# Gated attention and two feed-forward stages on one core: another written order for the first phase

## The chip, the cores and the metric

The program runs on one core of one Trainium2 chip. The core has a matrix engine (PE, with its weight loads shown as PEld), a vector engine (DVE), a scalar engine (ACT), a general engine (POOL) and a queue that issues transfers (SP). Each works through its own list of instructions in order; they meet only where one waits for a semaphore of another. The metric is the device time of one execution in microseconds (us), as the median of several; lower is better.

## The reference

Three stages follow each other. The first is an attention-like recurrence (an mLSTM cell) over 2 batches, 8 heads, 768 time steps and a head size of 40. Its output becomes 1536 tokens of 320 features. They go through a layer of four experts (320 to 1024 to 320), and then through a gated layer (320 to 1536 to 320).

```
for t in range(S):                                    # per batch b and head h
    m_new = max(f[t] + m, i[t])
    C = exp(f[t] + m - m_new) * C + exp(i[t] - m_new) * outer(v[t], k[t])
    n = exp(f[t] + m - m_new) * n + exp(i[t] - m_new) * k[t]
    y[t] = sigmoid(o[t]) * (C @ q[t]) / max(|n . q[t]|, 1)
x   = y as (B*S, H*D)
x   = sum over e of p[:, e] * (relu(x @ w1[e]) @ w2[e])        # p: normalised domain_probs
out = ((x @ w_a) * (x @ w_b)) @ w_out
```

## The kernel before

**Tiling.** The 768 steps are cut into six chunks (j = 0 to 5) of 128 steps. With two batches that gives twelve token tiles n = 2j and 2j + 1, each of 128 tokens. Every f32 operand of a matmul in the two feed-forward stages is split into a high half and a low half, and three products are added. The weights come in pieces: a piece is loaded, ACT copies its high half (L88), and POOL or DVE computes its low half (L90).

**Phase one** is what the change touches. It mixes two kinds of work on PE. One is the first expert blocks of the second stage, in *items*: 12 items for each chunk, numbered k = 0, 1, 2 and so on. An item's first part `a()` runs eight matmuls into `psa` (L201). ACT then evicts them as `hh` (L218, the high half), and DVE as `hl` (L219, the low half). Its second part `b()`, three matmuls per token tile into `psy` (L242 to L244), follows two items later. There are two `psa` buffers, so item k + 2 cannot start before DVE has done the `hl` of item k. Expert sums leave `psy` as `acc`: by ACT in the first blocks (L251), by DVE later (L253).

The other kind is the attention of the next chunk, in *events*. Chunk j is computed while the items of chunk j - 1 run, so what chunk 1 and the start of chunk 2 need runs beside the items of chunk 0, numbered 0 to 11. The events are:

- `gate1` to `gate4` and `gate_tail` compute the gates of a chunk: running maxima and sums by scans on DVE (L338 to L355), their high halves `zh` (`gate_hi`, L360 and L361), the low parts `LT` and `zx` (L367, L368), exponentials `ex` on ACT (L375, L376), a small product `eb` on POOL (L380), and on PE a transpose of `ex` (L386) and a product with `eb` (L389).
- `build_R` fills the right operand `Rr` of the gate products (L398). `weights_of` multiplies (L407), takes the exponential on ACT (L408) and masks it by a select on POOL (L409). `scores` multiplies queries by keys (L417). `s1b` multiplies the two on DVE (L425).
- `s2a` multiplies by the values (L435) and by the old state (L441). `s2b` normalises the result on DVE (L451 to L464) and leaves `x_t`. `weigh_k` (POOL, L473) and `state` (PE L485, DVE L487, POOL L490 and L491) carry the state `cbd` on.
- `s3a` transposes `x_t` on PE (L138 to L140). The third transpose reads the last 64 columns twice, so ACT copies them first (L496). `s3b` or `split_hi` and `split_lo` split the result into `xh` and `xl`, which the items read.
- `table` loads the table of the exponential or of the sigmoid on ACT (L526), and `o_gate` takes the sigmoid (L315).

**The order** of all this is written by hand and not moved by a scheduler. A list `ev` holds pairs of a time and an event. The loop over the items runs all events up to k, then the first part of item k, then the events up to k + 0.5, then the second part of item k - 2, then those up to k + 0.99:

```
for k in range(NI * NCH):
    until(k)
    stream.push(Item(...), lambda: until(k + 0.5))
    until(k + 0.99)
```

Every engine gets its instructions in the order in which this loop emits them. For the chunks 2 to 5 the events come from one list with an offset of 12 per chunk (`new`).

After phase one (from about 210 us) PE runs the remaining expert blocks and the gated layer without attention work.

Of the kernel before, what the change touches and what calls it, by code (L numbers as in the profile page):

```python
# [13 lines left out]
AF = mybir.ActivationFunctionType  # L14
# [3 lines left out]
DM = H * D  # L18
# [28 lines left out]
def mlstm_moe_kernel(ctx, tc, gates, qk, qc, kvo, dp, w1b, w2b, ident_d, bdmask_d, rsel_d, exp_d, out):  # L47
    nc = tc.nc
# [22 lines left out]
    def piece1(i, s, pool, lo_eng, apart=False):  # L71


        if s == 0:
            wblk[i] = (pool.tile([P, WB1], F32R, tag="wh", name=f"wh{i}"), pool.tile([P, WB1], F32R, tag="wl", name=f"wl{i}"))
        wh, wl = wblk[i]
        st = WB1 // NP1
        cs = slice(s * st, (s + 1) * st)
        if i < 3:
            at = (s if i == 0 else 8 + s if s < 2 else s) * st  # L80
            raw = sums[:, at:at + st]
        else:
# [46 lines left out]
    def split_hi(ps, c, o):  # L129
        nc.scalar.copy(xh[c][:, :, o:o + P], ps)  # L130
# [130 lines left out]
    with ExitStack() as c1:  # L261
# [7 lines left out]
        td = {}  # L269
# [61 lines left out]
        def gate1(j, eng):  # L331
            mr = a2.tile([G, P + 1], F32, tag="mr", name="mr")
            if j == 0:
                nc.gpsimd.memset(mr[:, 0:1], NEG)
            else:
                nc.scalar.copy(mr[:, 0:1], g_sb[j - 1]["mr"][:, P:])
            f, ig, m = g_sb[j]["gt"][:, 0], g_sb[j]["gt"][:, 1], mr[:, 1:]
            nc.vector.tensor_tensor_scan(m, f, ig, mr[:, 0:1] if j == 0 else g_sb[j - 1]["mr"][:, P:], op0=ALU.add, op1=ALU.max)  # L338
            cm = a2.tile([G, P], F32, tag="cm", name="cm")
            lf = a2.tile([G, P], F32, tag="lf", name="lf")  # L340
            eng.tensor_tensor(lf, f, mr[:, 0:P], op=ALU.add)
            eng.tensor_tensor(lf, lf, m, op=ALU.subtract)
            eng.tensor_tensor(cm[64:G], ig[64:G], m[64:G], op=ALU.subtract)
            g_sb[j].update(cm=cm, lf=lf, mr=mr)
# [133 lines left out]
        def state(n):  # L478
# [55 lines left out]
        w0, w1, w2 = ([piece1(i, f, wp0, nc.vector if LOENG[i][f] == "v" else nc.gpsimd) for f in range(NP1)] for i in range(3))  # L534
        V = nc.vector
# [56 lines left out]
        for n in range(2):  # L592
# [28 lines left out]
        go(w1[2:6])

        ev = [
            (0.5, gate2, 1), (0.5, gate_hi, 1, nc.vector.tensor_copy), (0.5, table, AF.Exp), (0.6, go, w0[7:]), (0.7, go, w0[6:]), (0.8, go, w1[6:]), (0.9, gate_tail, 0),
            (1.5, gate3, 1), (1.5, build_R, 2, V, 0, 4), (1.6, gate4, 1), (1.8, go, w1[0:2]), (1.9, go, w1[0:2]),
            (2.5, build_R, 2, V, 4, 8), (2.5, weigh_k, 0), (2.7, go, w2[:2]), (2.8, gate_tail, 1), (2.8, go, w1[2:4]), (2.9, go, w1[2:4]), (2.9, scores, 2, 0),
            (3.0, weigh_k, 1), (3.2, weights), (3.5, scores, 2, 1), (3.5, build_R, 3, V, 0, 4), (3.8, go, w1[4:6]), (3.9, weights_of, 2, 0), (3.9, go, w1[4:6]), (3.9, go, w2[2:4]),
            (4.5, weights_of, 2, 1), (4.5, build_R, 3, V, 4, 8), (4.6, table, AF.Sigmoid), (4.7, go, w1[6:8]), (4.8, s1b, 2, 0), (4.8, go, w1[6:8]), (4.9, o_gate, 1), (4.9, go, w2[4:6]),
            (5.0, state, 0), (5.2, go, w2[0:2]), (5.3, table, AF.Exp), (5.4, s1b, 2, 1), (5.4, go, w2[0:2]), (5.45, state, 1), (5.45, load_kvo, 3), (5.5, s2a, 2, 0), (5.6, s2a, 2, 1), (5.9, s2b, 2), (5.9, scores, 3, 0), (5.9, weights_of, 3, 0), (5.9, go, w2[6:8]), (5.95, go, w2[2:4]),
            (6.0, weigh_k, 2), (6.1, go, w2[2:4]), (6.4, gate1, 2, V), (6.6, go, w2[4:6]), (6.8, go, w2[4:6]), (6.9, s1b, 3, 0),  # L630
            (7.0, scores, 3, 1), (7.0, weights_of, 3, 1), (7.4, s3a, 2), (7.4, go, w2[6:8]), (7.45, gate2, 2), (7.5, weigh_k, 3), (7.6, go, w2[6:8]), (7.9, s1b, 3, 1), (7.9, s3b, 2),
            (8.3, gate_hi, 2, nc.scalar.copy), (8.5, s2a, 3, 0), (8.6, s2a, 3, 1), (8.9, s2b, 3),
            (9.4, state, 2), (9.5, gate3, 2), (9.9, state, 3), (10.0, build_R, 4, nc.gpsimd), (10.2, gate4, 2), (10.6, s3a, 3), (10.9, s3b, 3), (10.9, gate_tail, 2), (11.0, build_R, 5, nc.gpsimd),
        ]
# [207 lines left out]
```

## Time and profile before

| what | value |
|---|---|
| median of 3 runs | 647.97 us (647.9 to 648.02) |
| the profiled execution: device time | 647.9 us |
| the profiled execution: span of the trace | 646.2 us |
| PE busy | 626.6 us (97%) |
| PE weight loads busy | 568.6 us (88%) |
| DVE, ACT, POOL busy | 419.9 us (65%), 267.2 us (41%), 182.6 us (28%) |

The span runs from the first to the last instruction; the device time is 1.7 us longer. A row of the timeline gives the start and the length in us, the engine, the line of the kernel, the operation, output and inputs, and how many instructions of this kind follow each other there. A bracket at its end gives how long the engine stood idle before it, and what it waited for. Idle time of PE is the time to look for.

### The profile page before, as it was taken

What the parts mean: (1) busy time and instruction counts of PE and PEld (TensorE: products, weight loads), DVE (VectorE), ACT (ScalarE), POOL (GpSimd) and SP (SyncE); (2) the same over time, 40 slices, a digit from 0 to 9 for tenths busy, and PEclk for the clock granted to TensorE, in tenths of its full rate; (3) what the DMA queues carried; (4) which work ended last, traced back from release to release, by engine and by line L of the source; (5) the groups of instructions that cost most, each with busy time, mean ns of one, the idle gap of its engine ahead of it and who ended that gap; (6) DMA issues with size and microseconds to landing.
All of it is one profiled execution on the core that took longest, in us unless ns stands there. A gap on an engine that the chain in (4) does not pass through costs nothing.

```text
span 646.2 us, 10283 instructions
## 1 busy us (share of the span) xinstructions
PE 626.6 (97%) x3798; PEld 568.6 (88%) x3799; DVE 419.9 (65%) x860; ACT 267.2 (41%) x592; POOL 182.6 (28%) x217
## 2 busy tenths in 40 slices
PE   8887999999999999999999999999999999999997
PEld 6787989999999999999888988888888888888886
DVE  8986858576654244323587888888766776764343
ACT  6774454453614333232343443454544433332221
POOL 4595242525101111233243333322121222220000
PEclk9997999999999999999999999999999999999999
DMA  7873152615201122223122221211111111000003
GB/s 225 241 230 92 40 129 55 166 55 153 71 1 47 44 57 77 59 79 100 45 69 58 65 69 53 71 53 52 36 51 30 43 50 37 18 0 2 1 9 115
DMA packets 27487, 45.99 MB, mean 71 GB/s; under 512 B 3189, under 2 KB 17773, under 8 KB 27437
## 3 DMA queue, kind: packets, MB, share of 16 engines
q1 hardware_dynamic: 27437, 45.33, 25.2%
q8 instruction: 30, 0.49, 0.3%
q14 instruction: 20, 0.16, 0.1%
HBM read 43.35 MB, written 1.97 MB: 70 GB/s over the span
## 4 chain that ended last, share of the span: by engine, by line
PE 90%; DVE 5%; ACT 2%; issue 1%; POOL 1%; DVEq 0%; ACTq 0%; POOLq 0%
PE psa L201 37%; PE psy L242 12%; PE psy L244 11%; PE psy L243 11%; PE psb L201 10%; PE pt_y L435 3%; PE pt_c L417 2%; PE pt_i L441 1%; PE pt_a L407 1%; PE pt_u L485 1%; PE pt_e L389 1%; PE pt_x L140 1%; ACT hh L218 0%; ACT qs_t L301 0%; ACT acc L251 0%
## 5 line engine op out<-in xcount | busy, mean ns | idle before, releaser
L242 PE MATMUL psy<-wh,hh 128*128 128x320 f32 x528 | 166.3, 315 | 1.7 <-ACT acc L251 1.7
L244 PE MATMUL psy<-wh,hl 128*128 128x320 f32 x528 | 163.2, 309 | 0.0
L243 PE MATMUL psy<-wl,hh 128*128 128x320 f32 x528 | 163.1, 309 | 0.0
L201 PE MATMUL psa<-xh,wh 128*128 128x512 f32 (+1 forms) x504 | 149.6, 351 | 1.7 <-DVE hl L219 1.3
L201 PE MATMUL psa<-xh,wl 128*128 128x512 f32 (+1 forms) x504 | 147.1, 346 | 0.0
L219 DVE SCALAR_TENSOR_TENSOR hl<-psa,hh 128x256 fp32r<-128x256 f32 (+1 forms) x132 | 71.7, 543 | 111.7 <-ACT hh L218 111.2
L218 ACT ACTIVATE hh<-psa 128x256 fp32r<-128x256 f32 (+1 forms) x132 | 63.4, 480 | 187.4 <-PE psa L201 185.8
L242 PEld LDWEIGHTS psy<-wh,hh 128*128 128x128 f32 x528 | 99.8, 189 | 8.5 <-ACT acc L251 2.3
L243 PEld LDWEIGHTS psy<-wl,hh 128*128 128x128 f32 x528 | 99.6, 189 | 4.1
L201 PEld LDWEIGHTS psa<-xh,wl 128*128 128x128 f32 x504 | 90.2, 189 | 12.6
L244 PEld LDWEIGHTS psy<-wh,hl 128*128 128x128 f32 x528 | 99.4, 188 | 0.0
L201 PEld LDWEIGHTS psa<-xh,wh 128*128 128x128 f32 x504 | 89.1, 189 | 9.6 <-DVE hl L219 1.5
L201 PE MATMUL psa<-xl,wh 128*128 128x512 f32 (+1 forms) x336 | 88.9, 346 | 0.0
L122 POOL TENSOR_TENSOR wl<-tp,lf 128x272 fp32r<-128x272 f32 x48 | 38.8, 809 | 124.0 <-DVE tp L121 124.0
L201 PEld LDWEIGHTS psa<-xl,wh 128*128 128x128 f32 x336 | 58.4, 189 | 8.2
L228 DVE TENSOR_TENSOR g<-psa,bs 128x512 f32<-128x512 f32 x36 | 24.9, 691 | 50.2 <-PE psa L201 50.2
L119 POOL TENSOR_TENSOR lf<-lf,sq 128x272 f32<-128x272 f32 x48 | 37.5, 782 | 70.3 <-ACT wh L118 39.6
L90 POOL TENSOR_TENSOR wl<-raw,wh 128x352 fp32r<-128x352 f32 x28 | 26.4, 951 | 97.3 <-ACT wh L88 84.3
L229 ACT CAST hh<-g 128x512 fp32r<-128x512 f32 x36 | 22.3, 621 | 72.3 <-DVE g L228 72.3
L409 POOL TENSOR_SCALAR_AFFINE_SELECT w_t<-w_t 128x512 f32<-128x512 f32 x24 | 17.9, 752 | 83.0 <-ACT w_t L408 56.0
L230 DVE TENSOR_TENSOR hl<-g,hh 128x512 fp32r<-128x512 f32 x36 | 24.9, 693 | 24.7 <-ACT hh L229 24.7
L224 ACT COPY bs<-psb 128x512 f32<-128x512 f32 x36 | 21.2, 588 | 44.0 <-PE psb L201 43.9
(118 smaller groups left out, 893.0 us busy)
## 6 DMA issues: line engine op xcount, KB each, us to landing
raw<-in_w2b SPq DMA_DIRECT2D x48, 272.0 KB, 2.7
qk_t<-in_qk SPq DMA_DIRECT2D x16, 480.0 KB, 6.5
raw<-in_w1b SPq DMA_DIRECT2D x40, 176.0 KB, 2.3
acc<-in_w1b SPq DMA_DIRECT2D x24, 176.0 KB, 3.6
kvo_t<-in_kvo SPq DMA_DIRECT2D x10, 364.5 KB, 5.1
og_t<-in_kvo SPq DMA_DIRECT2D x6, 320.0 KB, 6.5
out<-acc SPq DMA_DIRECT2D x12, 160.0 KB, 1.8
qc_t<-in_qc SPq DMA_DIRECT2D x10, 180.0 KB, 3.1
```

The lines of the kernel that those rows point to most:

```text
L90: lo_eng.tensor_tensor(wl[:, cs], raw, wh[:, cs].bitcast(F32), op=ALU.subtract)
L119: nc.gpsimd.tensor_tensor(lf, lf, sq, op=ALU.mult)
L122: nc.gpsimd.tensor_tensor(wl[:, cs], tf, lf, op=ALU.add)
L201: nc.tensor.matmul(ps, l, r, start=(i == 0), stop=(i == len(prs) - 1))
L218: nc.scalar.activation(self.hh, ps, AF.Relu)
L219: nc.vector.scalar_tensor_tensor(self.hl, ps, 0.0, self.hh.bitcast(F32), op0=ALU.max, op1=ALU.subtract)
L228: nc.vector.tensor_tensor(g, ps, bs, op=ALU.mult)
L229: nc.scalar.copy(self.hh, g)
L230: nc.vector.tensor_tensor(self.hl, g, self.hh.bitcast(F32), op=ALU.subtract)
L242: nc.tensor.matmul(ps, lh, wh[:, off:off + DM], start=(fi == 0), stop=False)
L243: nc.tensor.matmul(ps, lh, wl[:, off:off + DM], start=False, stop=False)
L244: nc.tensor.matmul(ps, ll, wh[:, off:off + DM], start=False, stop=(fi == nf - 1))
```

## The change

Only phase one's written order changes. The copy of the last 64 columns of `x_t` becomes an event of its own, `s2c`, ahead of the transposes. The gate events of chunk 1 move behind the evictions of items 0 and 1, and those of chunk 2 from between two `s1b` steps to places next to them. `weigh_k(1)`, the mask of tile 3 and the product `eb` of chunk 2 move ahead of other work of POOL; `build_R(3)` moves behind other work of DVE. In chunks 2 to 5 the exponential's table is loaded an item earlier, right behind the sigmoid.

```diff
+        def s2c(n):
+            x = td[n]["x"]
+            nc.scalar.copy(x[:, DM:], x[:, 256:DM])
+
         def s3a(n):
             x = td[n]["x"]
-            nc.scalar.copy(x[:, DM:], x[:, 256:DM])
...
-        gate1(1, V)
...
-            (0.5, gate2, 1), (0.5, gate_hi, 1, nc.vector.tensor_copy), (0.5, table, AF.Exp), ...
+            (0.4, gate1, 1, V), (1.45, gate2, 1), (1.45, gate_hi, 1, nc.vector.tensor_copy), (0.5, table, AF.Exp), ...
...
-            (3.0, weigh_k, 1), (3.2, weights), (3.5, scores, 2, 1), (3.5, build_R, 3, V, 0, 4), ...
-            (4.5, weights_of, 2, 1), (4.5, build_R, 3, V, 4, 8), (4.6, table, AF.Sigmoid), ...
+            ... (2.85, weigh_k, 1), (2.9, go, w1[2:4]), (2.9, scores, 2, 0),
+            ... (4.8, s1b, 2, 0), (4.95, build_R, 3, V, 0, 4), ...
+            ... (5.45, state, 1), (5.45, build_R, 3, V, 4, 8), (5.45, load_kvo, 3), ...
-            ... (6.4, gate1, 2, V), (6.6, go, w2[4:6]), (6.8, go, w2[4:6]), (6.9, s1b, 3, 0),
+            ... (5.55, gate1, 2, V), (6.9, s1b, 3, 0), (6.95, s2c, 2),
-            ... (7.0, weights_of, 3, 1), (7.4, s3a, 2), ... (7.45, gate2, 2), ... (7.9, s1b, 3, 1), (7.9, s3b, 2),
+            ... (7.0, weights_of, 3, 1), (7.05, go, w2[4:6]), (7.1, go, w2[4:6]), (7.4, s3a, 2), ... (7.6, s1b, 3, 1), (7.9, s3b, 2), (7.95, gate2, 2),
-            (8.5, s2a, 3, 0), (8.6, s2a, 3, 1),
+            (8.2, s2a, 3, 0), (8.5, s2a, 3, 1),
-            (9.5, gate3, 2), (9.9, state, 3), (10.0, build_R, 4, nc.gpsimd), (10.2, gate4, 2), (10.6, s3a, 3),
+            (9.5, gate3, 2), (9.9, state, 3), (9.95, gate4, 2), (9.95, s2c, 3), (10.0, build_R, 4, nc.gpsimd), (10.6, s3a, 3),
...
-                (-4.0, table, AF.Sigmoid), (-3.5, o_gate, j), (-2.5, table, AF.Exp),
+                (-4.0, table, AF.Sigmoid), (-3.5, o_gate, j), (-3.45, table, AF.Exp),
-                (6.9, state, n0), (7.2, s3a, n0), ... (8.95, s2b, n1), (10.6, s3a, n1),
+                (6.9, s2c, n0), (6.9, state, n0), (7.2, s3a, n0), ... (8.95, s2b, n1), (9.95, s2c, n1), (10.6, s3a, n1),
```

On DVE, beside items 0 and 1 of chunk 0 (`hl` is the low half of an item, `wl` of a weight piece, L338 to L343 are `gate1` of chunk 1, L349 begins its `gate2`):

```order
 L90 TENSOR_TENSOR wl_138<-acc,wh_137 128x352
+L219 SCALAR_TENSOR_TENSOR hl<-psa,hh 128x256
 L338 SCALAR_TENSOR_TENSOR mr<-gt,mr 112x128
 L341 TENSOR_TENSOR lf<-gt,mr 112x128
 L342 TENSOR_TENSOR lf<-lf,mr 112x128
 L343 TENSOR_TENSOR cm<-gt,mr 48x128
+L90 TENSOR_TENSOR wl_138<-acc,wh_137 128x352
 L219 SCALAR_TENSOR_TENSOR hl<-psa,hh 128x256
 L349 TENSOR_SCALAR lf<-lf 112x128
```

The low half of item 0 moved ahead of the four steps of `gate1`, and a weight piece's low half and that of item 1 moved ahead of `gate2`.

On POOL, at the end of chunk 0's items (L490 and L491 end the two state updates of chunk 1, `eb` and `Rr` belong to chunk 2):

```order
 L490 TENSOR_TENSOR cbd_t<-cbd_t,dec 120x369
 L491 TENSOR_TENSOR cbd_t<-cbd_t 120x369
+L380 TENSOR_TENSOR eb<-expd,ex 16x2
 L398 TENSOR_TENSOR Rr_105<-zx,rsel 64x1024
-L380 TENSOR_TENSOR eb<-expd,ex 16x2
 L398 TENSOR_TENSOR Rr_106<-zx,rsel 64x1024
```

The small product `eb` moved ahead of the first fill of `Rr`; nothing else changed there.

On ACT, at items 8 to 10 of chunk 1, and alike in the two chunks behind it (`og_t` is the sigmoid, the numbers 526 and 529 are one line of the table's load before and after):

```order
 L218 ACTIVATE hh<-psa 128x256
 L315 ACTIVATE og_t<-og_t 128x640
-L218 ACTIVATE hh<-psa 128x256
-L526 ACT_TABLE_LOAD
-L526 ACTIVATE warm<-rmask 1x1
+L529 ACT_TABLE_LOAD
+L529 ACTIVATE warm<-rmask 1x1
+L218 ACTIVATE hh<-psa 128x256
 L251 ACTIVATE acc<-psy,pg 128x320 x2
```

The table's load moved from behind the eviction of item 9 to ahead of it. A few rows on, the copy L496 stands ahead of the eviction of item 10, where it stood behind it and behind a cast of 128 by 1024 (L301).

## Rows read from the trace of the kernel before

**Rows 1.** The page: its first line.

```profile
span 646.2 us, 10283 instructions
```

**Rows 2.** Waits of PE, whole span: total us, times, longest.

```profile
PE pt_x L140 <- ACT x_t L496: 4.7, 9, 1.2
PE pt_e L389 <- POOL eb L380: 2.8, 1, 2.8
PE psy L242 <- ACT acc L251: 1.7, 3, 0.6
```

**Rows 3.** Timeline, all engines, 18 to 25 us.

```profile
18.89 0.96 DVE L90 TENSOR_TENSOR wl<-acc,wh 128x352 fp32r<-128x352 f32 x1
...
19.46 0.38 ACT L218 ACTIVATE hh<-psa 128x256 fp32r<-128x256 f32 x1 [0.53 <-PE psa L201]
...
20.35 0.29 DVE L341 TENSOR_TENSOR lf<-gt,mr 112x128 f32<-112x128 f32 x1
...
21.32 0.42 DVE L219 SCALAR_TENSOR_TENSOR hl<-psa,hh 128x256 fp32r<-128x256 f32 x1
...
21.80 0.50 PE L201 MATMUL psa<-xh,wh 128*128 128x256 f32 x2 [1.31 <-DVE hl L219]
...
21.91 1.12 DVE L353 TENSOR_TENSOR_SCAN L<-rmask,lf 112x128 f32<-112x128 f32 x1
...
23.85 0.30 PE L386 MATMUL pt_e<-ident,ex 96*128 96x96 f32 x1
```

**Rows 4.** Timeline, all engines, 29 to 36 us.

```profile
30.97 0.65 POOL L409 TENSOR_SCALAR_AFFINE_SELECT w_t<-w_t 128x512 f32<-128x512 f32 x1
...
33.43 0.67 DVE L425 TENSOR_TENSOR w_t<-pt_c,w_t 128x512 f32<-128x512 f32 x1
...
34.21 1.09 PE L435 MATMUL pt_y<-kvo_t,w_t 128*128 128x82 f32 x8 [1.02 <-issue]
```

**Rows 5.** Timeline, all engines, 40 to 50 us.

```profile
42.73 0.90 DVE L342 TENSOR_TENSOR lf<-lf,mr 112x128 f32<-112x128 f32 x1
...
47.94 0.69 DVE L425 TENSOR_TENSOR w_t<-pt_c,w_t 128x512 f32<-128x512 f32 x1
...
48.68 1.12 PE L435 MATMUL pt_y<-kvo_t,w_t 128*128 128x82 f32 x8 [1.28 <-DVE w_t L425]
```

**Rows 6.** Chain that ended last, 50 to 66 us: start, length, what.

```profile
50.54 0.51 DVE y_t L451
...
57.14 2.30 POOL Rr L398
59.44 0.61 POOL eb L380
...
60.09 1.35 PE pt_e L389 x6
```

**Rows 7.** Windows of 1 us: busy time by engine, granted clock, DMA share, GB/s.

```profile
63.00:64.00 1.00, 1.00 (x6) 1.00 (x5) 0.03 (x1) 0.45 (x2) 0.00 (x0) 0.50 1.00 229
```

**Rows 8.** Timeline, all engines, 54 to 66 us: first matmuls of item 12.

```profile
64.77 0.40 PE L201 MATMUL psa<-xh,wh 128*128 128x256 f32 x2
```

**Rows 9.** Timeline, all engines, 84 to 98 us.

```profile
88.39 0.73 ACT L315 ACTIVATE og_t<-og_t 128x640 f32<-128x640 f32 x1
...
92.40 0.39 ACT L218 ACTIVATE hh<-psa 128x256 fp32r<-128x256 f32 x1 [3.28 <-PE psa L201]
...
92.81 0.49 DVE L464 TENSOR_TENSOR x_t<-x_t,og_t 128x320 f32<-128x320 f32 x1
92.81 1.28 ACT L526 ACT_TABLE_LOAD   x1
...
94.21 0.91 ACT L251 ACTIVATE acc<-psy,pg 128x320 f32<-128x320 f32 x2
...
94.76 0.19 PEld L242 LDWEIGHTS psy<-wh,hh 128*128 128x128 f32 x1 [0.76 <-ACT acc L251]
94.77 0.41 PE L242 MATMUL psy<-wh,hh 128*128 128x320 f32 x1 [0.56 <-ACT acc L251]
```

More of the change, by code (lines that the diff above doesn't have):

```diff
@@ L603, in mlstm_moe_kernel @@
         go(w0[2:3])
+        s2c(0)
         s3a(0)
@@ L611, in mlstm_moe_kernel @@
         warm_up(4)
+        s2c(1)
         s3a(1)
@@ L623, in mlstm_moe_kernel @@
         ev = [
-            (0.5, gate2, 1), (0.5, gate_hi, 1, nc.vector.tensor_copy), (0.5, table, AF.Exp), (0.6, go, w0[7:]), (0.7, go, w0[6:]), (0.8, go, w1[6:]), (0.9, gate_tail, 0),
+            (0.4, gate1, 1, V), (1.45, gate2, 1), (1.45, gate_hi, 1, nc.vector.tensor_copy), (0.5, table, AF.Exp), (0.6, go, w0[7:]), (0.7, go, w0[6:]), (0.8, go, w1[6:]), (0.9, gate_tail, 0),
             (1.5, gate3, 1), (1.5, build_R, 2, V, 0, 4), (1.6, gate4, 1), (1.8, go, w1[0:2]), (1.9, go, w1[0:2]),
-            (2.5, build_R, 2, V, 4, 8), (2.5, weigh_k, 0), (2.7, go, w2[:2]), (2.8, gate_tail, 1), (2.8, go, w1[2:4]), (2.9, go, w1[2:4]), (2.9, scores, 2, 0),
@@ L627, in mlstm_moe_kernel @@
-            (3.0, weigh_k, 1), (3.2, weights), (3.5, scores, 2, 1), (3.5, build_R, 3, V, 0, 4), (3.8, go, w1[4:6]), (3.9, weights_of, 2, 0), (3.9, go, w1[4:6]), (3.9, go, w2[2:4]),
-            (4.5, weights_of, 2, 1), (4.5, build_R, 3, V, 4, 8), (4.6, table, AF.Sigmoid), (4.7, go, w1[6:8]), (4.8, s1b, 2, 0), (4.8, go, w1[6:8]), (4.9, o_gate, 1), (4.9, go, w2[4:6]),
-            (5.0, state, 0), (5.2, go, w2[0:2]), (5.3, table, AF.Exp), (5.4, s1b, 2, 1), (5.4, go, w2[0:2]), (5.45, state, 1), (5.45, load_kvo, 3), (5.5, s2a, 2, 0), (5.6, s2a, 2, 1), (5.9, s2b, 2), (5.9, scores, 3, 0), (5.9, weights_of, 3, 0), (5.9, go, w2[6:8]), (5.95, go, w2[2:4]),
@@ L630, in mlstm_moe_kernel @@
[L630 to L633, printed above, removed]
+            (2.5, build_R, 2, V, 4, 8), (2.5, weigh_k, 0), (2.7, go, w2[:2]), (2.8, gate_tail, 1), (2.8, go, w1[2:4]), (2.85, weigh_k, 1), (2.9, go, w1[2:4]), (2.9, scores, 2, 0),
+             (3.2, weights), (3.5, scores, 2, 1), (3.8, go, w1[4:6]), (3.9, weights_of, 2, 0), (3.9, go, w1[4:6]), (3.9, go, w2[2:4]),
@@ new lines, in mlstm_moe_kernel @@
+            (4.5, weights_of, 2, 1), (4.6, table, AF.Sigmoid), (4.7, go, w1[6:8]), (4.8, s1b, 2, 0), (4.95, build_R, 3, V, 0, 4), (4.8, go, w1[6:8]), (4.9, o_gate, 1), (4.9, go, w2[4:6]),
+            (5.0, state, 0), (5.2, go, w2[0:2]), (5.3, table, AF.Exp), (5.4, s1b, 2, 1), (5.4, go, w2[0:2]), (5.45, state, 1), (5.45, build_R, 3, V, 4, 8), (5.45, load_kvo, 3), (5.5, s2a, 2, 0), (5.6, s2a, 2, 1), (5.9, s2b, 2), (5.9, scores, 3, 0), (5.9, weights_of, 3, 0), (5.9, go, w2[6:8]), (5.95, go, w2[2:4]),
@@ new lines, in mlstm_moe_kernel @@
+            (6.0, weigh_k, 2), (6.1, go, w2[2:4]), (5.55, gate1, 2, V), (6.9, s1b, 3, 0), (6.95, s2c, 2),
+            (7.0, scores, 3, 1), (7.0, weights_of, 3, 1), (7.05, go, w2[4:6]), (7.1, go, w2[4:6]), (7.4, s3a, 2), (7.45, go, w2[6:8]), (7.5, go, w2[6:8]), (7.6, weigh_k, 3), (7.6, s1b, 3, 1), (7.9, s3b, 2), (7.95, gate2, 2),
+            (8.3, gate_hi, 2, nc.scalar.copy), (8.2, s2a, 3, 0), (8.5, s2a, 3, 1), (8.9, s2b, 3),
+            (9.4, state, 2), (9.5, gate3, 2), (9.9, state, 3), (9.95, gate4, 2), (9.95, s2c, 3), (10.0, build_R, 4, nc.gpsimd), (10.6, s3a, 3), (10.9, s3b, 3), (10.9, gate_tail, 2), (11.0, build_R, 5, nc.gpsimd),
@@ L645, in mlstm_moe_kernel @@
                 (4.2, s2a, n0, 0), (4.5, s2a, n0, 1), (4.6, weigh_k, n1), (4.95, s2b, n0),
-                (5.4, s1b, n1, 0), (6.2, s1a, n1, 1), (6.9, state, n0), (7.2, s3a, n0), (7.4, s1b, n1, 1), (7.6, state, n1), (7.9, s3b, n0),
-                (8.2, s2a, n1, 0), (8.5, s2a, n1, 1), (8.95, s2b, n1), (10.6, s3a, n1), (10.9, s3b, n1),
+                (5.4, s1b, n1, 0), (6.2, s1a, n1, 1), (6.9, s2c, n0), (6.9, state, n0), (7.2, s3a, n0), (7.4, s1b, n1, 1), (7.6, state, n1), (7.9, s3b, n0),
+                (8.2, s2a, n1, 0), (8.5, s2a, n1, 1), (8.95, s2b, n1), (9.95, s2c, n1), (10.6, s3a, n1), (10.9, s3b, n1),
             ]
```

## The prediction

> **What bounds the kernel now.** The device time of the profiled execution is 647.9 us, its span 646.2 us [rows 1], so 1.7 us lie around it; the median of the runs, 647.97, is the same to 0.07 us. PE is busy in 97% of the span (the table above), so a new order can only win back what PE stands idle, and the time in which its clock is low. I read the waits of PE first. The first three rows name what phase one loses in many places: the third transpose waits for the copy of `x_t` 9 times, 4.7 us in all; PE waits once 2.8 us for `eb`; and `psy` waits three times, 1.7 us, for ACT's `acc` [rows 2]. The timeline adds three single waits beside chunk 0 and 1: 1.31 us for `hl` of item 0 [rows 3], 1.02 us ahead of `pt_y` of tile 2 [rows 4] and 1.28 us ahead of that of tile 3 [rows 5]. The second of these is put down to "issue", but the row of `w_t` ahead of it ends at 34.10, so it is a wait for DVE too [rows 4]. Last, the clock: after the wait for `eb` PE runs at a granted 0.50, which is 1.2 of 2.4 GHz [rows 7], until item 12 begins at 64.77 [rows 8]. From there to the end of phase one only the two waits that repeat per chunk are left, and behind phase one PE does not wait enough to matter.
>
> **The change, step by step.** No work is added or removed; every step is a place in an order. I count how much earlier PE gets, with minus for later. A matmul's bracket runs from the modelled end of the one before, and that end overlaps the next start. The weight load of the wait at 94.77 stood 0.76 where its matmul shows 0.56 [rows 9], so I take each wait as 0.16 longer than the waits say.
>
> *Item 0's low half ahead of `gate1`.* `hh` is ready at 19.46 + 0.38 = 19.84, and DVE is free of a weight piece at 18.89 + 0.96 = 19.85 [rows 3]. `hl` then starts near 19.9 in place of 21.32, and item 2 follows item 1 at 21.80 - 1.31 - 0.16 = 20.33. What is late next is `ex` of chunk 1, for which PE waits right behind items 2 and 0. Two pieces of work now stand ahead of its scan on DVE: a weight piece (0.96 at most) and `hl` of item 1 (0.42). The scan starts near 23.2 and not at 21.91. It took 1.12 there beside a low half on POOL; without it I take less than half, since like steps take 0.29 alone and 0.90 beside POOL [rows 3, 5]. From its end at 23.03 to the transpose at 23.85 are 0.8, so PE starts that near 24.4 [rows 3]: **-0.55** (bounds: -1.3 with the scan at its full length, -0.1 with the weight piece at half length). So this stall is moved and not removed: PE stands about 2.0 us.
>
> *`weigh_k(1)` and the mask ahead, `build_R(3)` behind.* The product `w_t` of tile 2 was at 33.43 behind two fills of `Rr`, although its mask was done at 31.62 [rows 4]. Without them it runs near 31.4 and is done at 32.0, before PE gets there. The wait of 1.02 + 0.16 is gone, less 0.3 because the second half of tile 2 then has to wait behind `hl` of item 5, whose eviction stands behind a table's load. **+0.9** (0.5 to 1.2).
>
> *`gate1(2)` and `gate2(2)` out from between the two products of tile 3.* The row of 47.94 stands behind seven gate steps that run beside POOL's low halves; one of them shows 0.90 for what alone takes 0.29 [rows 3, 5]. At their new places the product of tile 3 is done near 44.2, and PE gets to it near 45.3: the 1.28 + 0.16 is gone. The copy of `x_t` (tile 2) stands ahead of its transposes: 0.39 + 0.16, where 0.39 is what the 4.7 us leave beside the others. **+2.0** (1.3 to 2.1).
>
> *Copy of tile 3 and `eb`.* The copy costs PE 1.2 us, the longest of its kind [rows 2], with 0.16 some 1.4; it now stands ahead of a cast and an eviction: **+1.4**. PE is by then 3.8 us ahead and reaches the product with `eb` at about 53.5. The chain of waits tells when `eb` comes: `y_t` starts at 50.54, the state updates end at 57.14, a fill of `Rr` takes 2.30, `eb` 0.61 [rows 6]. The fill is out of the way: 2.30 saved. The chain starts when DVE comes to `y_t`, which now stands behind `gate2(2)`; its steps run beside POOL until about 47.3, and `y_t` starts near 48.0, 2.5 earlier. So `eb` is there at 59.44 + 0.61 - 2.30 - 2.5 = 55.25, and PE still waits 1.8. Counted at this place, all steps so far make 60.09 - 55.25 = **4.8 us** (4.0 to 6.3; the upper end if PE does not wait for `eb` at all).
>
> *The clock.* From 60.09 to 64.77 are 4.68 us of work at half the clock [rows 6 to 8]; at full clock it takes 2.34 to 2.7, since the smallest matmuls do not halve. **+2.0**, if the clock stays up over a wait of 1.8 us. A row shows it up over 1.31 and 1.28 [rows 3, 5], and down after 1.2 and 2.8 with two small matmuls between them [rows 2, 6, 7]. My wait is nearer to the first, so I take the gain whole; the lower bound is 0.
>
> *Chunks 2 to 5.* The copies: of the 4.7 us, 0.39 and 1.2 are counted above, 3.1 are left in 7 waits [rows 2], with 0.16 each 4.2. The first copy of a chunk needs an `x_t` that is old; the second needs one that ends at 92.81 + 0.49 = 93.30, and ACT gets to it near 93.75 [rows 9]. The table: at 88.39 + 0.73 ACT is through with the sigmoid and stands until 92.40, 3.28 in all; the load of 1.28 fits there, `acc` (two, 0.91) moves from 94.21 to about 92.8, and `psy` at 94.77 no longer waits [rows 9]. 1.7 in three waits [rows 2], with 0.16 each 2.2. Sum **+6.2**, 4.2 and 2.2 less 0.2 for first matmuls that start slowly either way (4.8 to 6.4). It hides under a cover of 3.28 us per chunk on ACT.
>
> A page speaks against that step. The Trainium skill, "ScalarE: Activation LUTs", section "What ACT_TABLE_LOAD costs", says that each switch to another set costs 1.28 us and a drain of 1.38 us behind it. Here the load starts at 92.81, and `acc` at 94.21, with a dummy of 0.2 us ahead of it: 0.1 of its 1.4 us is left over [rows 9], so this trace shows no such drain. By the page the sum would be 1.0 us smaller, by the row it stays.
>
> *Sum:* 4.8 + 2.0 + 6.2 = 13.0 us; 647.9 - 13.0 = 634.9, and with the median the same. I say **635 us**.
>
> **Rivals.**
>
> *The clock falls at one of the two waits that are left.* PE stands about 2.0 us near 22 to 24 and 1.8 us near 53 to 55, both longer than any wait over which it stayed up. Each fall would cost what it costs now, about 2.0 to 2.3: 637.0 for the second, 639.2 for both.
>
> *DVE stays stretched.* `gate1(2)` runs at its new place beside the end of four low halves of POOL. I have it take 1.8 us; if all four steps take 0.9 [rows 5], `x_t` of tile 2 comes 1.6 later, the transposes wait for it about 1.3, and `y_t` of tile 3 shifts with it: 636.3, and with `gate2(2)` at full length too 637.3. The overlap of the rows speaks for some of it.
>
> *A table's load that holds ACT longer than its row.* If ACT stood as long again as the load takes, 1.28 us, `hh` of item 9 beside chunk 0 would come 1.3 later; its `hl` had 0.3 to spare, and the state update and `eb` behind it are late by 1.0: 636. The row against it is the start of `acc` at 94.21. The page of the Trainium skill named above would bring this.
>
> *The copies block ACT: slower.* `s2c` now stands ahead of evictions, and ACT works strictly in order. Were `x_t` late when ACT gets to the second copy, `hh` of item 10, then its `hl`, then item 12 would wait. That happens in five chunks and needs 2.6 us of lateness in each to eat 13 us; beyond that the kernel is slower, 649.5 at 2.9 us. DVE's rows put `x_t` at 93.30 and ACT at 93.75, so this has a margin of 0.4 us and not a deficit.
>
> *The stalls only move.* If what ends a wait is always a neighbour of what was named, only the chunks 2 to 5 gain part: 645 to 647. Item 0 is a case of it, the others are not by their rows.
>
> **How the numbers follow.** Forecast with its own bounds, 633 to 637: 0.62. Clock: 0.17. Stretched DVE beyond the forecast: 0.10, and the long load 0.02, both within 637.5. Stalls that only move: 0.06. Slower: 0.03. The forecast and the first three rivals reach from 632.5, where the bounds of `eb` and of the copies are met together, to 639.5; that holds about 0.85. A change of 0.2% (1.3 us) is about what a measurement of this kernel tells from none. Faster by more than that: 0.95; within it, from the moved stalls and the copies that are a little late: 0.02; slower: 0.03.
>
> **What would show it.** PE's waits should have no row of L140 for the copy, and none of `psy` for `acc`. The wait for `hl` of item 0 should be gone and one of about 2 us for `ex` should stand at the transpose L386 near 24. `pt_y` should not wait for `w_t`. The product with `eb` should start near 55, after a wait of 1 to 2 us, and item 12 near 58. The granted clock should be full from there; a stretch at 0.50 makes the prediction too low by 2. Each of the chunks 2 to 4 should be about 1.9 us shorter. The prediction is wrong if ACT waits for DVE ahead of L496, or if the gate steps of chunk 2 still take 0.9 each.

## The result: 640.7 us, faster by 1.2%, and less than forecast

The changed kernel takes 640.73 us in the median of four runs (638.94 to 642.22), the kernel before 648.0 in runs beside it (647.9 to 648.79). The ratio is 0.988, 95% interval 0.986 to 0.991. The profiled execution took 638.94 us with a span of 637.2, so again 1.7 lie around it. The forecast gain of 13.0 us came out as 7.3 in the medians and 9.0 in the profiled executions. The median lies outside the range that was given.

### The profile page after: what moved, and what is told of

Read it like the earlier page. It is cut to its first block, busy times and chain, and to the rows that moved or that the text cites. A ratio compares the mean times of both kernels' runs of the same rounds, so it can differ in the third digit from the quotient of the medians.

```text
span 637.2 us, 10280 instructions
## 1 busy us (share of the span) xinstructions
PE 624.7 (98%) x3799; PEld 569.1 (89%) x3799; DVE 421.6 (66%) x860; ACT 266.7 (42%) x592; POOL 182.4 (29%) x217
## 4 chain that ended last, share of the span: by engine, by line
PE 90%; DVE 6%; ACT 2%; issue 1%; POOL 0%; DVEq 0%; ACTq 0%; POOLq 0%
PE psa L201 37%; PE psy L242 12%; PE psy L244 11%; PE psy L243 11%; PE psb L201 10%; PE pt_y L435 3%; PE pt_c L417 2%; PE pt_i L441 1%; PE pt_a L407 1%; DVE qs_t L304 1%; PE pt_u L485 1%; ACT wh L88 0%; DVE hl L219 0%; PE pt_e L389 0%; PE pt_x L138 0%
## 5 line engine op out<-in xcount | busy, mean ns | idle before, releaser
L409 POOL TENSOR_SCALAR_AFFINE_SELECT w_t<-w_t 128x512 f32<-128x512 f32 x24 | 18.2, 763 | 78.0 <-ACT w_t L408 56.9
```

## The profile after

The page of the changed kernel: its first line, the busy time of the engines, and the granted clock in 40 slices of 16 us.

```profile
span 637.2 us, 10280 instructions
...
PE 624.7 (98%) x3799; PEld 569.1 (89%) x3799; DVE 421.6 (66%) x860; ACT 266.7 (42%) x592; POOL 182.4 (29%) x217
...
PEclk9898999999999999999999999999999999999999
```

Against [rows 1] the span is 9.0 shorter, and PE is busy for nearly as long as before (624.7 us for 626.6). Two slices show a lowered clock, the second (16 to 32 us) and the fourth (48 to 64 us), where the rows of before had one low stretch, at [rows 7]. The low stretches add up to the same in both traces: 57.8 to 64.6 us before, 26.2 to 29.6 and 60.3 to 63.7 after, 6.8 us each. PE's waits in the changed kernel (total us, times, longest):

```profile
PE pt_e L389 <- POOL eb L380: 2.5, 1, 2.5
PE pt_e L386 <- ACT ex L376: 2.0, 1, 2.0
PE pt_x L138 <- DVE x_t L464: 1.4, 2, 1.0
PE pt_w L522 <- POOL wz L517: 1.4, 1, 1.4
PE psb L201 <- DVE xh L135: 0.6, 1, 0.6
PE psa L201 <- ACT xh L130: 0.4, 1, 0.4
```

Of [rows 2] the copy (4.7 us, 9 times) and `acc` (1.7 us) are gone. `eb` is still there with 2.5 for 2.8, and `ex` of chunk 1 (2.0) and `x_t` of tile 2 (1.0 of the 1.4) have come in. The timeline of the changed kernel at the places of [rows 3 to 9]; its columns are those of the rows before.

```profile
20.34 0.50 PE L201 MATMUL psa<-xh,wh 128*128 128x256 f32 x2
...
24.43 0.30 PE L386 MATMUL pt_e<-ident,ex 96*128 96x96 f32 x1 [1.99 <-ACT ex L376]
...
42.38 0.86 DVE L459 TENSOR_TENSOR dn_t<-y_t,dn_t 128x8 f32<-128x8 f32 x1
...
43.51 0.95 DVE L463 TENSOR_TENSOR x_t<-y_t,dn_t 128x320 f32<-128x320 f32 x1
44.50 0.49 DVE L464 TENSOR_TENSOR x_t<-x_t,og_t 128x320 f32<-128x320 f32 x1
...
45.13 0.30 PE L138 MATMUL pt_x<-ident,x_t 128*128 128x128 f32 x1 [1.01 <-DVE x_t L464]
...
51.50 0.49 DVE L451 TENSOR_TENSOR y_t<-pt_i,ET 128x328 f32<-128x328 f32 x1
...
52.24 1.28 ACT L529 ACT_TABLE_LOAD   x1
...
53.64 0.36 ACT L218 ACTIVATE hh<-psa 128x256 fp32r<-128x256 f32 x1
...
57.11 0.96 POOL L491 TENSOR_TENSOR cbd_t<-cbd_t 120x369 f32<-120x369 f32 x1
57.18 5.74 DVE L304 TENSOR_TENSOR qs_t<-qk_t,qs_t 40x512 fp32r<-40x512 f32 x2
...
58.02 0.64 POOL L380 TENSOR_TENSOR eb<-expd,ex 16x2 f32<-16x2 f32 x1
...
58.63 3.74 POOL L398 TENSOR_TENSOR Rr<-zx,rsel 64x1024 fp32r<-64x1024 f32 x2
...
58.72 0.79 PE L389 MATMUL pt_e<-eb,expd 16*120 16x2 f32 x6 [2.52 <-POOL eb L380]
...
62.20 0.63 PE L201 MATMUL psa<-xh,wh 128*128 128x256 f32 x2
...
62.85 0.41 DVE L133 TENSOR_TENSOR xl<-pt_x,xh 128x256 fp32r<-128x256 f32 x1
...
63.31 0.69 PE L201 MATMUL psa<-xl,wh 128*128 128x256 f32 x2
...
86.04 0.73 ACT L315 ACTIVATE og_t<-og_t 128x640 f32<-128x640 f32 x1
86.79 1.28 ACT L529 ACT_TABLE_LOAD   x1
...
91.43 0.24 ACT L496 COPY x_t<-x_t 128x64 f32<-128x64 f32 x1
...
92.80 0.27 PE L140 MATMUL pt_x<-ident,x_t 128*128 128x128 f32 x1
```

Follow PE's lead over the kernel before, that is, by how much earlier it starts the same matmul. Item 2 starts at 20.34 against 21.80 [rows 3], a lead of 1.46; at the transpose L386 it is -0.58, where the forecast had -0.55. At the product with `eb` it is 60.09 - 58.72 = 1.37 [rows 6], where the forecast had 4.8; at item 12 it is 64.77 - 62.20 = 2.57 [rows 8], and as item 12 still runs at half clock there and its third product comes only at 63.31, behind `xl` of tile 3, it shrinks to 1.62 by item 13 (67.29 before, 65.67 after). From there it grows to 9.0 at the end. So the early part gave 1.6 for 6.8, and the chunks 2 to 5 gave 7.3 for 6.2. In the last rows the table's load stands right behind the sigmoid, and the third transpose follows with no bracket, as forecast.

The clock in the changed kernel, in stretches of 1 us (us, then busy time and count of PE, PEld, DVE, ACT, POOL; then granted clock, DMA share, GB/s):

```profile
23.00:24.00 1.00, 0.00 (x0) 0.00 (x0) 0.90 (x4) 0.33 (x2) 0.07 (x1) 1.00 0.71 211
...
27.00:28.00 1.00, 1.00 (x6) 1.00 (x6) 0.87 (x1) 0.19 (x1) 1.00 (x2) 0.50 0.79 244
...
57.00:58.00 1.00, 0.00 (x0) 0.00 (x0) 0.97 (x2) 0.30 (x1) 0.92 (x2) 1.00 0.00 0
...
61.00:62.00 1.00, 1.00 (x6) 1.00 (x5) 1.00 (x1) 1.00 (x2) 1.00 (x1) 0.50 0.00 0
```

PE stands still in the first and third row, and behind each wait its clock is at 0.50, 1.2 of 2.4 GHz, while PE is fully busy. By the shares in the rows around them the stretches at 0.50 reach from 26.2 to 29.6 and from 60.3 to 63.7, so they begin 1.8 and 1.6 us behind the end of the wait.

## The experiments

The dummy matmuls in some kernels multiply zeros into a part of the buffer `pt` that nothing reads; they compute nothing, and all other work is kept. Every time is a median, with the range of its runs.

**Is the late part worth what was forecast?** The kernel before with only the list of chunks 2 to 5 changed; the changed kernel with only that list undone; and the late copies without the table.

```diff
# late_only: before, and
-   (-2.5, table, AF.Exp)
+   (-3.45, table, AF.Exp), (6.9, s2c, n0), (9.95, s2c, n1)
    ...                     # s3a itself copies for the tiles of chunks 0 and 1 only
# early_only: after, with these lines as before
# late_copies: late_only, with
+   (-2.5, table, AF.Exp)
```

> The kernel before, with only the chunks 2 to 5 changed: the copy of x_t ahead, the exponential's table right behind the sigmoid. Theory: these two steps are worth what the trace of the changed kernel gains between item 13 and the end of phase one, 9.0 - 1.6 = 7.25 us, and need nothing of the rest: 640.7 us, clock as before. Rival one: the forecast's 6.2 us was the right size and the rest came from the early part: 641.8. Rival two: they only pay on top of the early part: 644 or more.

Measured: 640.78 (640.06 to 641.01), ratio 0.988 (0.9865 to 0.9895).

> The changed kernel with chunks 2 to 5 as before: only the order beside chunks 0 and 1 is changed. Theory: this part is worth 1.6 us when the clock falls twice as in the profiled execution of the changed kernel (646.3), and nothing or a small loss when it falls for longer (up to 648 or 649), so its runs should spread as those of the changed kernel did. Rival: the forecast's 6.8 us (641.2) with runs close together.

Measured: 646.2 (644.64 to 651.23, ten runs), ratio 0.998 (0.996 to 1.0002). The runs order themselves by the mean granted clock: 644.65 at 0.996 to 0.997, 646.0 at 0.994, 648.0 at 0.992, 651.2 at 0.987.

> The kernel before, with only the copies of chunks 2 to 5 moved ahead of their transposes; the exponential's table stays in its old place. The two parts of the late edit together gave 7.25 to 7.6 us against a forecast of 4.2 for the copies and 2.2 for the table, less 0.2. Theory (each wait costs its bracket and 0.16, and the wait of psy 0.3 as its first two matmuls start slowly): copies 4.2 to 4.5, time 643.5 to 643.9, and the waits show 1.7 us for acc as before. Rival (the copies were under-sized, since ACT also finishes the eviction behind them later): copies 5 or more, 643.0 or less. A second rival: without the table's step ACT is busy when the copy is due, and waits for acc grow: 645.

Measured: 643.33 (642.15 to 644.12), ratio 0.992 (0.990 to 0.994), 5.1 below the kernel before beside it. PE's waits of the first and the third of these kernels:

```profile
PE pt_x L140 <- ACT x_t L496: 1.6, 2, 1.2
```

```profile
PE psy L242 <- ACT acc L251: 1.7, 3, 0.6
PE pt_x L140 <- ACT x_t L496: 1.6, 2, 1.2
```

The copies leave the two waits of chunk 1 and nothing else, and only the table's step removes `acc`. The late edit alone gains as much as the whole change; the early edit alone gains about 2 us, less than the spread of its runs, and its interval does not exclude no gain. The copies give about 5.1 of the late gain (forecast 4.2), the table the other 2.5 (forecast 2.2); by the leads of the traces from item 13 on it is 4.8 and 2.4. The Trainium skill, "ScalarE: Activation LUTs", section "What ACT_TABLE_LOAD costs", adds a drain of 1.38 us to each load of another set. The changed kernel's trace shows none: beside chunk 0, where the rival of the long load had put it, the load starts at 52.24 and the eviction behind it at 53.64, 1.40 later, with a dummy of 0.20 between. The 2.5 us alone would not decide it, as load and drain, 2.66 us together by that page, would still fit into the 3.28 that ACT stood [rows 9].

**Is it the clock?** 16 dummy matmuls ahead of the transpose of chunk 1, and 20 ahead of the product with `eb`, keep PE working while it waits. As a control, 24 in the second place in the kernel before.

```diff
# fill_both: after, and in gate_tail
+   for _ in range(16 if j == 1 else 0): matmul(pt[:, 256:512], wz[:, 0:P], wz[:, 0:256])
    transpose(pt[:, 0:96], ex, ident)
+   for _ in range(20 if j == 2 else 0): matmul(pt[:, 256:512], wz[:, 0:P], wz[:, 0:256])
# before_fill: before, with 24 in the second place
```

> The changed kernel with dummy matmuls on zeros into an unused part of the same buffer, 16 ahead of the first late transpose of ex and 20 ahead of the product with eb, so that PE is busy while it waits. Nothing is earlier by it. Theory: the clock falls because PE stands idle at these two places; kept busy it stays full, which gives back about 1.5 us at the first and 1.7 at the second: 635.7, mean clock near 1.00, and runs close together. Rival: the waits alone are the loss and the clock is not: 640.7 as now, or more by what the dummies overshoot.

Measured: 637.34 (637.28 to 637.39), ratio 0.983 (0.981 to 0.984): 3.4 below the changed kernel, and the spread of 3.3 between its runs is down to 0.1.

> The kernel before with 24 dummy matmuls on zeros between the transpose of ex and the product with eb of chunk 2, where PE waits 2.8 us. Nothing else changes. Theory: the clock no longer falls there, which gives back the 2.0 us of the prediction's clock term (2.3 if all of the 4.7 us halve): 645.7 to 646.0 and mean clock near 1.00. Rival: item 12 is bound by DVE and POOL there anyway, so a full clock only turns into a wait for xl: 647 or more.

Measured: 645.83 (645.62 to 647.37), ratio 0.997 (0.996 to 0.998), 2.5 below the kernel before. One of its six runs, the one at 647.37, had a mean clock of 0.997, so the clock fell in it all the same; where, no trace shows. Two windows of 2 us of the first kernel, columns as above:

```profile
26.00:28.00 2.00, 2.00 (x19) 2.00 (x19) 1.90 (x3) 0.00 (x0) 2.00 (x3) 1.00 1.04 305
...
60.00:62.00 2.00, 0.68 (x6) 0.47 (x5) 1.97 (x3) 0.57 (x1) 0.89 (x1) 1.00 0.00 0
```

and its timeline where item 12 runs:

```profile
57.23 0.79 PE L393 MATMUL pt_e<-eb,expd 16*120 16x2 f32 x6 [0.37 <-POOL eb L380]
...
61.83 0.50 PE L201 MATMUL psa<-xl,wh 128*128 128x256 f32 x2 [1.32 <-DVE xl L133]
```

The clock is at 1.00 in both places. But PE, now faster, stands 1.32 us for `xl` of tile 3: a wait that the low clock had hidden. The control puts the fall in the kernel before at 2.2 us (profiled executions) to 2.5 (medians), close to the forecast's 2.0; that term had the right size for a fall that did not go away.

**Can the waits be filled with real work instead?** `gate_tail` of both chunks is put later in the changed kernel, so that PE gets to it when `ex` and `eb` are there.

```diff
# tail12: after, and
-   (2.8, gate_tail, 1), (10.9, gate_tail, 2)
+   (3.6, gate_tail, 1), (12.95, gate_tail, 2)
```

> The changed kernel with gate_tail of chunk 1 at 3.6 in place of 2.8 and of chunk 2 at 12.95 in place of 10.9: PE does other work first, and the transposes and products come when ex and eb are ready. Theory: both waits (2.0 and 2.5 us) go, and with them the two falls of the clock (about 3.2): 638.9 - 7.7 = 631.2, runs close together. Rival: the stalls only move, to who reads the result of the transposes or to the next late product on DVE: 636 or more.

Measured: 641.38 (639.92 to 644.04), ratio 0.990 (0.987 to 0.9925): nothing gained. Its waits:

```profile
PE psa L201 <- DVE xl L133: 5.0, 1, 5.0
...
PE pt_a L407 <- ACT dec L393: 1.5, 1, 1.5
```

The wait for `eb` moved on to `xl` of tile 3, which DVE has not done either, and grew to 5.0. The other wait shows something about the clock as well; the row of its matmul, and a window of 1 us behind it:

```profile
29.75 0.80 PE L407 MATMUL pt_a<-Rr,LT 112*128 112x512 f32 x1 [1.52 <-ACT dec L393]
```

```profile
30.00:31.00 1.00, 1.00 (x4) 0.91 (x5) 0.90 (x4) 1.00 (x4) 1.00 (x2) 0.50 0.19 69
```

It is PE's only wait over 0.5 us between 18 and 30 us. It lasted 1.52, and right behind it the clock stood at 0.50 for 3.4 us.

**What holds `xl` of tile 3?** DVE works at that time on `qs_t` (L304), beside POOL's two fills of `Rr`. The second fill is put off; then also the subtraction, behind `xl`; or `eb` is put back behind the first fill.

```diff
# fill_r5: fill_both, and
-   (11.0, build_R, 5, nc.gpsimd)
+   (13.6, build_R, 5, nc.gpsimd)
# fill_r5_split: fill_r5, and
-   (-1.5, split_qk, n0, 0)
+   (-1.5 if j > 2 else -1.05, split_qk, n0, 0)
# fill_eb_back: fill_both, and
-   (9.95, gate4, 2), ... (10.0, build_R, 4, nc.gpsimd)
+   (10.0, build_R, 4, nc.gpsimd), (10.2, gate4, 2)
```

> As fill_both (changed kernel with dummy matmuls in both waits, 637.34 us), and the second fill of Rr of chunk 2 on POOL moved from 11.0 to 13.6, away from the first. With eb ahead, the two fills run back to back, 3.74 us, and the subtraction of qs_t on DVE (L304), which takes 0.69 alone, lasts until they end; the low half xl of tile 3 and with it item 12 (a wait of 1.32) come behind it. Theory: DVE gets free 1.9 us earlier, and the wait of 1.32 goes: 636.0. Rival: DVE is held by something else there: 637.3.

Measured: 636.77 (636.66 to 636.83), ratio 0.983 (0.981 to 0.9845).

> As fill_r5, and the split of the queries of tile 4 on DVE moved behind the low half of tile 3. Theory: the low half of tile 3 no longer stands behind the subtraction at all, so item 12 does not wait; what waits instead is the score product of tile 4, which has its operand at the end of the first fill: 635.8 to 636.2, no better than fill_r5 by more than 0.3. Rival: the subtraction, now later, holds back the gate steps behind it and gives 0.5 us or more back: 636.5 or more.

Measured: 636.23 (636.17 to 636.43), ratio 0.982 (0.980 to 0.983). In both the wait for `xl` is gone from the trace. PE's lead at item 13 grows from 3.2 in fill_both to 4.9 and 5.4, but both lose 1.2 again between items 15 and 17, right behind the second fill's new place.

> As fill_both (637.34 us), with the exponentials and eb of chunk 2 back behind the first fill of Rr. eb comes 2.3 us later. Theory: item 12 waits for xl of tile 3 whatever eb does, and stood 1.3 us for it, so only what is left of the 2.3 shows: 638.2 to 638.4. Rival: eb ends the wait that counts, as the prediction had it, and all of the 2.3 shows: 639.6. Both with the clock kept up by the same dummy matmuls, unless 20 of them are too few for the longer wait; then the clock shows it.

Measured: 639.43 (637.99 to 639.5), ratio 0.986 (0.9845 to 0.9875). The run at 637.99 had a mean clock of 0.999, the three others 0.997. With the clock kept, `eb` behind the fill costs 0.65; the rest of the 2.1 goes with the clock. The profiled execution, the one at 637.99, shows the wait for `eb` back at 2.6 in spite of the dummies, and yet the clock at 1.00 throughout; of the others there is no trace. Its row, and a window behind it:

```profile
59.50 0.68 PE L393 MATMUL pt_e<-eb,expd 16*120 16x2 f32 x5 [2.58 <-POOL eb L380]
```

```profile
60.00:61.00 1.00, 1.00 (x9) 0.98 (x9) 0.06 (x1) 0.31 (x2) 1.00 (x1) 1.00 0.47 41
```

**The gates, back where they were.** `gate1(2)` back to item 6, in the kernel with dummies; and the gates of chunk 1 back ahead of item 0's low half, in the changed kernel.

```diff
# fill_g1: fill_both, and
-   (5.55, gate1, 2, V)
+   (6.4, gate1, 2, V)
# gates1_back: after, and
+   gate1(1, V)            # ahead of the list, as before
-   (0.4, gate1, 1, V), (1.45, gate2, 1), (1.45, gate_hi, 1, nc.vector.tensor_copy)
+   (0.5, gate2, 1), (0.5, gate_hi, 1, nc.vector.tensor_copy)
```

> As fill_both, with gate1 of chunk 2 back at 6.4, behind the low half of item 6, where it stood before the change. Theory: at its new place it holds up the normalisation of tile 2, whose result comes 1.4 us too late for the transposes; back there, that wait goes, but the product of tile 3 stands behind it again. DVE is busy throughout, so what is saved ahead of the transposes is lost again ahead of eb: 637 within 0.6. Rival: the wait is a plain loss of 1.2 us: 636.1. Other rival: the order of before is worse by the 1.3 us wait that it had there: 638.6.

Measured: 636.26 (636.22 to 636.37), ratio 0.982 (0.980 to 0.983): 1.1 below fill_both. The wait for `x_t` falls from 1.4 to 0.4.

> The changed kernel, with the gates of chunk 1 back where they stood: gate1 ahead of item 0's low half, gate2 behind it. PE then waits 1.31 us for that low half again, and not 2.0 us for ex. Theory: over 1.3 us the clock stays up, over 2.0 it falls, so this gives back the 0.55 us by which the moved stall is longer and the 1.5 us at half the clock: 638.6, with a higher mean clock than the changed kernel. Rival: only the 0.55 counts: 640.2.

Measured: 637.98 (636.68 to 638.4), ratio 0.984 (0.982 to 0.985): 2.7 below the changed kernel. Its waits, and a window of 2 us:

```profile
PE pt_e L389 <- POOL eb L380: 2.5, 1, 2.5
...
PE psa L201 <- DVE hl L219: 1.3, 1, 1.3
```

```profile
26.00:28.00 2.00, 2.00 (x19) 2.00 (x18) 1.97 (x4) 0.10 (x1) 2.00 (x3) 1.00 0.87 264
```

With the wait of 1.3 for `hl` in place of 2.0 for `ex`, the clock stays up beside chunk 0. It still falls behind the wait for `eb`, from 56.9 to 63.7, as long in all as in the profiled execution of the changed kernel. These two executions differ by 0.54 (638.94 and 638.4); the rest of the 2.7 goes with the lower clock of the changed kernel's other runs (0.988 and 0.992, against 0.995 and 0.997 here).

**All of it together.**

```diff
# best1: fill_r5_split with fill_g1's edit
# best2: best1 without the first dummies, and gate_tail(1) at 3.6, go(w1[2:4]) at 3.65 and 3.7
# best3: best1 without the first dummies, with gates1_back's edit, and 18 dummies for 20
```

> fill_r5_split (636.23) and fill_g1 (636.26) together: dummy matmuls in both waits, second fill of Rr later, low half of tile 3 ahead of the split of the queries, gate1 of chunk 2 back behind the low half of item 6. Theory: the two gains lie at different places on DVE and add: 637.34 - 1.11 - 1.08 = 635.2. Rival: DVE is the bound from item 6 to item 12, so that one gain uses up the other: 636.

Measured: 635.57 (635.39 to 635.58), ratio 0.9805 (0.979 to 0.982).

> best1 with no dummies in the first wait; instead the transpose of ex of chunk 1 comes at 3.6, behind item 3, and ACT's casts of two weight pieces, which wait for their transfer, come behind its copies. PE does items instead of waiting. Theory: PE gains up to 2.0 us until about item 4, of which DVE, busy from item 6 on, gives back part: 633.8 to 635.0. Rival: what stands behind the copies on ACT and POOL comes late instead, and the time stays at that of best1 or gets worse.

Measured: 636.06 (635.88 to 636.14), ratio 0.981 (0.980 to 0.983). Real work in the first wait is no gain over dummies: it is 0.5 slower than best1, and its trace has new waits of 0.8 to 1.0 us, for `w_t` and `xh`.

> The fastest version so far, with the gate events of chunk 1 back in their old places, without the dummy matmuls ahead of the transpose L386 of chunk 1, and with 18 instead of 20 ahead of the product with eb. Theory (the moved wait of 2.0 us costs its excess over the old wait, 0.55, whatever the clock does): a wait of 1.3 us for hl of item 0 is back, the clock stays at 1.00 through 30 us, and the time is 635.57 - 0.55, so 634.8 to 635.2. Rival (the 2.7 us that the same edit gave in the changed kernel were all clock and further falls): nothing is left where the clock is kept, 635.4 to 635.8. A second rival: the old wait of 1.3 us lets the clock fall in some executions, which would spread the runs over more than 1 us.

Measured: 634.93 (634.41 to 635.17), ratio 0.979 (0.977 to 0.981). It is the fastest kernel here. Its timeline of DVE, POOL and PE where `eb` is made:

```profile
54.22 0.40 DVE L133 TENSOR_TENSOR xl<-pt_x,xh 128x256 fp32r<-128x256 f32 x1
...
55.18 0.18 POOL L380 TENSOR_TENSOR eb<-expd,ex 16x2 f32<-16x2 f32 x1
55.33 1.89 POOL L400 TENSOR_TENSOR Rr<-zx,rsel 64x1024 fp32r<-64x1024 f32 x1
...
55.45 0.78 PE L391 MATMUL pt_e<-eb,expd 16*120 16x2 f32 x6
...
57.61 1.39 DVE L304 TENSOR_TENSOR qs_t<-qk_t,qs_t 40x512 fp32r<-40x512 f32 x2 [2.66 <-ACT qs_t L301]
```

`eb` is done at 55.36 and PE takes it at 55.45; `xl` is long there, and L304 takes 1.39 behind the fill where it took 5.74 in the changed kernel.

## Why the prediction failed, step by step

**The step that failed** is *The clock*: "My wait is nearer to the first, so I take the gain whole." The clock fell at both of the waits that the prediction itself had left, 2.0 us for `ex` (called right) and 2.5 for `eb` (called 1.8). It was the first rival, which gave 639.2 for both; the profiled execution took 638.94, the median 640.73. That 638.94 comes so near is luck, as with the clock kept the kernel takes 637.34 and not 634.9. The mean granted clock of the four runs, 0.995, 0.992, 0.992 and 0.988 for 638.94, 640.72, 640.73 and 642.22, says that the time beyond 638.94 is time at half clock; at which places, no trace shows. With PE kept busy 3.4 us came back. So the rows were read wrongly at one point: the clock was up over the waits of 1.31 and 1.28 [rows 3, 5], and down after 2.8 [rows 6, 7]; I took a wait of 1.8 to 2.0 for the former kind, without a row between. Nor does the length of a wait alone decide it: the clock fell behind 1.52 in tail12 and stayed up over 2.58 in fill_eb_back. What else does is open.

By the leads, the terms of the early part came out so in the profiled execution: first step -0.58 (forecast -0.55), the fall of the clock beside chunk 0 -1.6 (0), mask +1.2 (0.9), gates of chunk 2 +0.6 (2.0), copy of tile 3 +1.5 (1.4), `eb` +0.3 (about 1.0), clock behind `eb` +0.2 (the 2.0 of the failed step). They add up to 1.6 for 6.8, and 3.3 of the 5.2 between are the clock's two places. With the waits filled 1.6 of it comes back between the profiled executions (638.94 and 637.34); at full clock the wait for `xl` takes its place.

**Item 0's low half, -0.55.** Right at its place (-0.58), but the clock fell behind the moved wait: undoing the step kept it up there and gave 2.7 in the changed kernel. From best1 to best3, where the clock is up either way, it is 0.64, the forecast's size; best3 also has no first dummies and two fewer in the second place, so the 0.64 holds these too.

**The mask, +0.9.** `pt_y` of tile 2 went from a lag of 2.15 (1.5 of it from the clock) to one of 0.96: +1.2, at the upper bound. The wait of [rows 4] is gone.

**`gate1(2)` and `gate2(2)`, +2.0.** The wait of [rows 5] is gone, but `x_t` of tile 2 was late (done at 44.99), and PE waited 1.01 for it. The steps of `gate1(2)` were not much longer than forecast, 2.2 us from 38.42 to 40.59 for 1.8, and three of the four took 0.29 each. What they pushed beside POOL's work was the normalisation behind them: L458, L459 and L463 took 0.66, 0.86 and 0.95, where they had taken 0.17, 0.17 and 0.49. Two of these in the kernel before:

```profile
39.10 0.17 DVE L459 TENSOR_TENSOR dn_t<-y_t,dn_t 128x8 f32<-128x8 f32 x1
...
39.54 0.49 DVE L463 TENSOR_TENSOR x_t<-y_t,dn_t 128x320 f32<-128x320 f32 x1
```

So the rival of the stretched DVE came true in its price (1.3; fill_g1 measures 1.1), but at other steps than it named. That this loss would be given back at `eb`, as was expected of fill_g1, did not happen.

**The copy of tile 3, +1.4.** The lead goes from -0.39 at item 9 to 1.08 at the transpose of `ex`, +1.47: right.

**`eb`, 4.8 at its product.** It was 1.37, because the clock, `x_t` and `y_t` (51.50 for a forecast of 48.0) were late in turn; `eb` was done at 58.66 for 55.25. In best3, with these mended, it is done at 55.36, so the chain was read nearly rightly: `y_t` starts at 48.64 for 48.0, and `eb` itself takes 0.18 and not 0.61, which makes up for most of that. What I did not price is what moving `eb` does to DVE. In the kernel before, `eb` stood between the two fills, and the subtractions L304 came through behind the first:

```profile
56.71 3.28 DVE L304 TENSOR_TENSOR qs_t<-qk_t,qs_t 40x512 fp32r<-40x512 f32 x2 [0.49 <-ACT qs_t L301]
```

Now the fills follow each other, and L304 takes 5.74, for 3.28 before and 1.39 alone. One by one in the trace, the first subtraction runs from 57.18 to 58.62, 0.55 beyond the end of the state update L491 at 58.07, and the second from 58.63 to 62.92, 0.55 beyond the end of the second fill at 62.37; alone each takes 0.69. `xl` of tile 3 stands behind them. Putting the second fill and then the subtractions out of the way gave 0.57 and 0.54.

The Trainium skill, "SBUF — State Buffer", section "Who interferes with whom", says that a VectorE operation with two inputs in SBUF and a GpSimd operation that reads SBUF exclude each other, so that the second to start stands until the first is through. The trace agrees in that both subtractions end just behind POOL's work, and that `eb`, which starts while the first runs, takes 0.64 for 0.18 alone and ends 0.05 behind it. The second subtraction got no turn between the two fills either. So here these two engines meet not only at semaphores, as was said at the start. It is a page that would have named this kind of wait ahead of time.

**Chunks 2 to 5, +6.2.** Right in mechanism, 7.3 by the leads and 7.6 by late_only. The size was off: I took 0.2 off for matmuls that start slowly either way, where such a start is part of what a wait costs. One row shows it: at 94.77 PE stood 0.56 by its bracket [rows 9], but the lead of the changed kernel grows from 2.35 at the matmul ahead (93.93 before, 91.58 after) to 3.18 at the one behind (95.02 and 91.84), by 0.83. The 0.16 that I added to each wait does not follow from its row either, where 0.76 less 0.56 is 0.20. The copies' margin of 0.4 us on ACT held; the slower case did not come.

**The account.** From the median to 634.93 there are 5.8 us: 3.4 kept clock (640.73 to 637.34), 1.8 for `gate1(2)` and L304 (to 635.57), 0.6 with the first step undone. That best3 lands on the forecast is no proof of the forecast's sum: its late part gains about 1.4 more than forecast, its early part some 0.9 less (648.4 - 634.93 = 13.5 in all, of which 7.6 late leaves 5.9 for 6.8). Its own trace says it in more detail: a lead of 6.7 at item 13, of which 1.2 goes right behind the second fill's new place, and 7.3 more by the end.

## What to carry to other kernels

Where an order is rewritten, sum the stalls that stay as carefully as those that go: a wait that is moved and grows from 1.3 to 2.0 us can cost more in clock than in standing (of the 2.7 us here, 0.55 is standing). If PE must wait, give it matmuls that compute nothing, and see first which wait appears behind. Moving one small operation on POOL ahead of fills also moves the fills: look at what the vector engine reads beside them.

## What was not expected of the hardware

- In the profiled executions PE's clock fell behind single waits of 1.52 (tail12), 1.99 and 2.52 us, and stayed up over waits of 1.28 to 1.32; but it also stayed up over one of 2.58, behind dummies (fill_eb_back). The two stretches at 0.50 in the changed kernel lasted 3.4 us each, the one in the kernel before 6.8. The runs of the changed kernel with a mean clock of 0.992 took 1.8 us longer than the one with 0.995.
- The spread between executions was the clock's: 3.3 us in the changed kernel, 0.1 with the waits filled, at a mean clock of 1.0.
- L304, 1.39 us for two alone, took 5.74 beside POOL's work. Of that work the fills were no longer than alone (3.74 for two, 1.89 for one), but `eb` took 0.64 for 0.18. In the kernel before, a fill that started behind the first subtraction took 2.30 [rows 6].
